# A token mixer of an FFT, a block MLP and a gated feed-forward net on one core: four chunks take their gate without a way by HBM, one sum reads PSUM, and phase one is spread over more time

## The chip, the core and the metric

The kernel runs on one core of a Trainium2 chip. Its engines are TensorE (PE: matrix products into the PSUM banks; PEld is its loading of weights), VectorE (DVE), ScalarE (ACT), GpSimd (POOL) and SyncE (SP), which here issues almost every DMA. Each engine takes its own instructions in a fixed order and waits at the head for what an instruction needs. The metric is the device time of one execution in microseconds: 1838.61 us is the median of three runs of the kernel before (1837.89 to 1843.89).

## The reference

8192 tokens of 448 channels are normalized (xn). A spectral branch s takes a Fourier transform over the tokens, a small two-layer complex MLP in four blocks of 112 channels on each frequency, a soft threshold, and the transform back. A feed-forward branch g is a gated GELU net of 1792 hidden units. The output is x + s * silu(g):

```python
xn = _layernorm(x)
Xf = rfft2(xn)                        # over 8192 tokens
hr, hi = relu(block products of Xf with w1 + b1)
or_, oi_ = softshrink(block products of h with w2 + b2, 0.01)
s = irfft2(or_ + 1j * oi_)
g = _silu((_gelu(xn @ w_gate) * (xn @ w_up)) @ w_down)
return x + s * g
```

## The kernel before

All products run in float16 pairs (a high and a low part), so that one product of the reference is three matmuls on PE. Two streams of work share the engines.

**The feed-forward stream** (`ffn`, `chunk`, `unit`, `down2`) is cut into 16 chunks of 512 tokens (`NG`), each passed twice: the first pass (p = 0) does 8 of the 14 blocks of 128 hidden units, the second (p = 1) the other 6. The first pass leaves its partial result in HBM (`prt`), the second reads it back into buffers `pt`. The tokens come transposed from HBM (`xts` into `xta`, `xtb`). A unit is two blocks of hidden units; its products come by a scheme with seven products in place of eight, called a1, a5, a6, a2, a3, a7 and a4 (in the last unit of a second pass a7 comes before a3). Their sums build up in PSUM banks `bx` (two of them) and `by`: a1, a6, a7 and a4 add into the same bank `bx`, and between two of them ACT or DVE must have read the bank's state. After a7 that is `c22` (L1097): ACT copies the bank into `v`, and then DVE or POOL adds `u` (product a5's sum) to it. a4 may add into the bank only when that copy is done. a4 is issued after the next unit's a1 and a5, or, for the last unit of a second pass, right behind a3. After a4, ACT's GELU, DVE's products and sums (`wt`, `h`) and the down products `down2` into banks `bd` and `by` follow.

At the end of a second pass the 512 x 448 result comes in four quarters (`QS`, L1213). `ended2` (L1284) adds the last sum to `pt`, takes `th` = tanh on ACT, makes the gate (th + 1) * q on DVE and writes it to HBM (`gsp<-th`). The buffers `th` are a ring of two (L490); the first pass uses the same ring for its way to HBM (`ended`, L1337, `prt<-th`). A buffer is free when its store has landed.

**The spectral stream** has three phases. Phase one (`chunk1`, L600) normalizes a chunk, writes its factors to `xts` and does the first stage of the transform into `t1`; chunk c starts at T1 + (c - 2) * DT in the plan. Phase two (`phase2`, L1725) is 64 groups of 4 frequencies and one block: transform, MLP, threshold, first stage back, into `t2`. Phase three (`phase3`, L1791) is 32 pieces of 256 tokens: `load3` (L1746) loads `u`, `mt`, `x` and the gate `g` (from `gsp`), `tiles3` (L1763) does six matmuls `bf<-u,mt` of 448 columns, multiplies on DVE with the gate, adds x (DVE or POOL) and stores (`out<-g`). Chunk 15 has no way by HBM even before: its four tiles are kept in `s4` with x in `x4l`, and `ended2` finishes them.

**Order.** The instruction streams are made ahead of time by a planner (`Pace`): every task is a generator, and the planner's own costs decide in which order tasks issue to each engine, and, for an add on SBUF alone (`Either`, L204), whether DVE or POOL takes it. Phase two is given the plan time up to `END2` = 1480, phase three up to `END3` = 1780. All instructions are recorded in one helper, so every row of the profile has its line, L199; tiles tell them apart.

Of the kernel before, what the change touches and what calls it, by code (L numbers as in the profile page):

```python
# [14 lines left out]
ALU = mybir.AluOpType  # L15
# [358 lines left out]
def afno_geglu_kernel(ctx, tc, x, gu, wd, mlp, b1, b2, c_m, c_mt, c_small, out):  # L374
# [22 lines left out]
    def ring(pool, shape, dt, name, bufs):  # L397
        return Ring(pace, pool, shape, dt, name, bufs)
# [88 lines left out]
    V1 = ring(fp, [128, 512], F32, "v1", 1)  # L487
    V2 = ring(fp, [128, 512], F32, "v2", 2)
    GL = ring(fp, [128, 512], F32, "gl", 1)
    TH = ring(fp, [128, D], F32, "th", 2)  # L490

    def load_x(c):
        x4 = EV["x4", c] = yield from X4.get()
# [146 lines left out]
            if c + 1 < NG + PL:  # L640
                yield ev("phase", c)

    T1, DT = 84.0, 40.0


    def gu_loads(fs, again):
# [346 lines left out]
                         start=first and e == 0 and n == 0, stop=last and e == 1 and n == len(seq) - 1,  # L993
                         skip_group_check=True)

    state = {}

    def scaled(p, f0):

# [23 lines left out]
    def unit(p, i, f0, h, xa):  # L1023
# [72 lines left out]

        def c22():  # L1097
            m["v2"] = yield from V2.get()
            S.copy(m["v2"], m["X"])
            pace.set(m["ev2"])  # L1100
            yield
            B.tensor_add(m["v2"], m["v2"], m["p5"])
            U5.put(m["p5"])
            yield
            pace.set(m["ec22"])
# [100 lines left out]
    def blk(a, hh, dd):  # L1206

        return a[:, hh:CH:2, DH * dd:DH * dd + DH]

    def chunk_of(a, i):  # L1210
        return a[i].rearrange("p (a d) -> p a d", a=CH)
# [31 lines left out]
    def add2(i, q, bank_):  # L1243

        yield ev("pt", i, q)
        t = EV["ptb", i, q]
        V.scalar_tensor_tensor(t, part(bank_, 128, 2, DH), cB[1], t, op0=ALU.mult, op1=ALU.add)
        yield

    def down2(i, h, last):  # L1250
# [30 lines left out]

        state["tail"] = tail

    def ended2(i, qq, b, R):  # L1284

        yield from add2(i, qq, b)
        if R:
            R.put(b)
        else:
            done("u3", i)  # L1290
        q = EV["ptb", i, qq]
        tf = yield from TH.get()
        th = tf.rearrange("p (a d) -> p a d", a=2)
        S.activation(th, q, AF.Tanh)
        yield
        if i < NG - 1:
            V.scalar_tensor_tensor(th, th, 1.0, q, op0=ALU.add, op1=ALU.mult)
            PT.put(q)
            yield
            Q.dma_start(blk(chunk_of(gsp, i), *qq), th)  # L1300
            TH.put(tf)
            EV["gn", i] = EV.get(("gn", i), 0) + 1
            if EV["gn", i] == 4:
                done("gsp", i)
            return
        for a in range(qq[0], CH, 2):
            yield ev("s4", a)
        s4, x4 = (blk(t, *qq) for t in state["last"])
        V.tensor_tensor(s4, q, s4, op=ALU.mult)
        V.scalar_tensor_tensor(th, th, 1.0, s4, op0=ALU.add, op1=ALU.mult)  # L1310
        V.tensor_add(th, th, x4)
        PT.put(q)
        yield
        Q.dma_start(blk(ov[:, CH * i:CH * i + CH, :], *qq), th)
        TH.put(tf)
# [78 lines left out]
    def chunk(p, i):  # L1394
# [10 lines left out]
        if p == 1 and nxt:  # L1405
            pace.spawn(xt_load(nxt[1], "a", nxt[0]))
        xa = EV["xta", p, i]
        if p == 1:
            pace.spawn(pt_loads(i))
        prev = None  # L1410
        for u in range(nf // 2):
            six, last = unit(p, i, 2 * u, h, xa)
# [350 lines left out]
    def tiles3(c):  # L1763
        yield ev("l3", c)
        t = EV["l3t", c]
        u2, mt = t[0:2]
        o2 = t[3] if c < 2 * NG - 2 else None
        for a in range(2):
            b = yield from BF.get()
            p = part(b, 128, D)  # L1770
            three(p, mt[:, a], u2[:, a, 0:D], u2[:, a, D:2 * D])
            yield
            if o2 is None:
                S.activation(state["last"][0][:, 2 * (c % 2) + a, :], p, AF.Copy, scale=cF)
                BF.put(b)
                yield
                done("s4", 2 * (c % 2) + a)
                continue
            V.scalar_tensor_tensor(o2[:, a, :], p, cF, o2[:, a, :], op0=ALU.mult, op1=ALU.mult)
            BF.put(b)  # L1780
            yield
            B.tensor_add(o2[:, a, :], o2[:, a, :], t[2][:, a, :])
            yield
        P3["u2"].put(u2)
        P3["mt"].put(mt)
        if o2 is not None:
            P3["x2"].put(t[2])
            Q.dma_start(ov[:, 2 * c:2 * c + 2, :], o2)
            P3["g2"].put(o2)

    def phase3():  # L1791
        r2.close()
        p3 = ctx.enter_context(tc.tile_pool(name="p3", bufs=1, side="right"))
        state["last"] = [p3.tile([128, CH, D], F32, name=n) for n in ("s4", "x4l")]
        for name, shape, dt, bufs in (("u2", [128, 2, 2 * D], F16, 3), ("mt", [128, 2, 3, 128], F16, 3),
                                      ("x2", [128, 2, D], F32, 3), ("g2", [128, 2, D], F32, 3)):
            P3[name] = ring(p3, shape, dt, name, bufs)
        n3 = 2 * NG
        order = list(range(n3))
        t0 = pace.now  # L1800
        dt = (END3 - t0 - 12.0) / n3
        pace.spawn(load3(order[0]))
        pace.spawn(load3(order[1]))
        Q.dma_start(state["last"][1], xv[:, CH * (NG - 1):, :])
        for k, c in enumerate(order):
            yield t0 + 10.0 + k * dt
            if k + 2 < n3:
                pace.spawn(load3(order[k + 2]))
            pace.spawn(tiles3(c))
# [162 lines left out]
```

## Time and profile before

| what | value |
|---|---|
| time, median of 3 runs | 1838.61 us (1837.89 to 1843.89) |
| the profiled execution | 1839.94 us |
| its span in the trace | 1838.2 us |
| PE busy | 1779.2 us (97%), 15649 matmuls |
| DVE busy | 1417.2 us (77%) |
| ACT busy | 1100.8 us (60%) |
| POOL busy | 477.4 us (26%) |
| DMA | 287.78 MB, some 300 GB/s from about 1520 to 1745 us |

A row of a timeline gives the start and the length in us, the engine, the line, the operation, the tiles as out<-in, the shape, a count, and in square brackets how long the engine was idle ahead of it and what ended that. A row of waits gives who waited for whom: total us, times, the longest. A row of grouped instructions gives, behind the first bar, the busy us and the mean ns of one. A row of windows gives the busy us of each engine in that stretch with the number of instructions, the granted PE clock, the busy share of the DMA engines and GB/s.

### The profile page before, as it was taken

To read this page: it belongs to the slowest core of one execution; us is meant where nothing else is said; L and a number is where in the kernel's file an instruction comes from. 1 tells how busy PE (TensorE), PEld (TensorE's weight loads), DVE (VectorE), ACT (ScalarE), POOL (GpSimd) and SP (SyncE) were. 2 spreads that over 40 slices of the span, in tenths; PEclk is the share of its full clock that TensorE was granted. 3 is DMA by queue.
4 is the path that set the end of the run, shared out by engine and by line. 5 is a ranking of instruction groups with operands and counts; after the bars stand their busy time and mean duration, and the time that the engine had idled before them with its cause. 6 is when DMAs were issued, how large, how long until landed. Compare 5 with 4: busy or idle time off the path is not lost. (4 is left out here: it accounts for less than half of the span.)

```text
span 1838.2 us, 39083 instructions
## 1 busy us (share of the span) xinstructions
PE 1779.2 (97%) x15649; PEld 1427.1 (78%) x15649; DVE 1417.2 (77%) x2503; ACT 1100.8 (60%) x2105; POOL 477.4 (26%) x544
## 2 busy tenths in 40 slices
PE   6999999999999999999999999999999999999997
PEld 3446677666777777887877899999999997788886
DVE  7876888777876656666767788888888877888877
ACT  4645666556665545566766777777677753444453
POOL 3232334225232112000000232333223322322222
PEclk9899999999999999999999999999999999999999
DMA  6454665676636623314236544434354359999972
GB/s 248 140 160 128 185 199 158 205 237 191 177 113 174 180 70 98 66 48 96 56 102 190 137 113 117 117 88 115 92 116 110 91 134 313 299 306 304 304 217 71
DMA packets 345654, 287.78 MB, mean 157 GB/s; under 512 B 231840, under 2 KB 312736, under 8 KB 345472
## 3 DMA queue, kind: packets, MB, share of 16 engines
q1 hardware_dynamic: 345328, 285.26, 54.4%
q8 instruction: 122, 2.00, 0.4%
q14 instruction: 60, 0.49, 0.1%
q10 hardware_dynamic: 144, 0.03, 0.0%
HBM read 129.47 MB, written 106.61 MB: 128 GB/s over the span
## 5 line engine op out<-in xcount | busy, mean ns | idle before, releaser
L199 PEld LDWEIGHTS <-wt 128*128 128x128 f16 x9350 | 911.3, 98 | 188.0 <-issue 23.3
L199 PE MATMUL bx<-xta,wt 128*128 128x256 f16 (+1 forms) x3843 | 475.4, 275 | 5.6 <-ACT th L199 3.6
L199 PEld LDWEIGHTS <-h 128*128 128x128 f16 x2688 | 257.8, 98 | 139.4 <-DVE h L199 8.5
L199 PE MATMUL bd<-dw,h 128*128 128x448 f16 (+1 forms) x1920 | 346.6, 329 | 8.3 <-DVE h L199 5.7
L199 PE MATMUL by<-xtb,wt 128*128 128x256 f16 x2080 | 251.5, 273 | 0.8 <-ACT u L199 0.8
L199 PE MATMUL by<-xta,wt 128*128 128x256 f16 (+1 forms) x1347 | 180.1, 283 | 4.9 <-DVE wt L199 3.1
L199 ACT COPY v<-bx 128x512 f32<-128x512 f32 x208 | 121.5, 584 | 99.2 <-PE bx L199 98.4
L199 POOL TENSOR_TENSOR wt<-wt 128x256 f32<-128x256 f32 x94 | 77.3, 823 | 285.0 <-DVE wt L199 263.4
L199 PE MATMUL bx<-xtb,wt 128*128 128x256 f16 x1040 | 131.6, 274 | 3.4 <-ACT v L199 3.4
L199 DVE TENSOR_TENSOR u<-by,u 128x512 f32<-128x512 f32 x104 | 71.4, 686 | 67.7 <-PE by L199 67.4
L199 ACT ACTIVATE u<-u,fc 128x512 f32<-128x512 f32 (+1 forms) x118 | 77.6, 669 | 54.9 <-DVE u L199 54.6
L199 PE MATMUL bd<-dw,wt 128*128 128x224 f16 (+1 forms) x816 | 97.1, 268 | 6.0 <-DVE pt L199 6.0
L199 POOL TENSOR_TENSOR zs<-t,zs 112x256 f16<-112x256 f32 (+1 forms) x36 | 30.7, 852 | 267.9 <-ACT zs L199 254.4
L199 ACT CAST h<-wt 128x512 f16<-128x512 f32 (+1 forms) x128 | 68.5, 537 | 37.6 <-DVE wt L199 25.1
L199 ACT COPY u<-by 128x512 f32<-128x512 f32 x104 | 60.9, 585 | 42.0 <-PE by L199 34.5
L199 DVE SCALAR_TENSOR_TENSOR pt<-bd,fb,pt 128x448 f32<-128x448 f32 x96 | 64.0, 678 | 27.3 <-PE bd L199 26.8
L199 PE MATMUL bf<-w2t,wn 112*128 112x112 f16 x1512 | 84.9, 213 | 0.0
L199 ACT ACTIVATE th<-bd,fb 128x448 f32<-128x448 f32 x62 | 39.2, 632 | 71.9 <-PE bd L199 50.1
L199 ACT COPY u<-bx 128x512 f32<-128x512 f32 x104 | 60.8, 585 | 35.7 <-PE bx L199 34.2
L199 PEld LDWEIGHTS <-wn 112*128 112x128 f16 x1512 | 80.5, 98 | 2.1
L199 ACT ACTIVATE th<-pt 128x448 f32<-128x448 f32 x64 | 36.8, 575 | 73.9 <-DVE pt L199 55.3
L199 DVE TENSOR_TENSOR v<-by,v 128x512 f32<-128x512 f32 x104 | 71.0, 683 | 9.9 <-PE by L199 9.2
(206 smaller groups left out, 3107.5 us busy)
## 6 DMA issues: line engine op xcount, KB each, us to landing
wst<-in_gu SPq DMA_DIRECT2D x22, 704.0 KB, 5.0
xts<-sx SPq DMA_DIRECT2D x32, 480.0 KB, 3.4
x<-in_x SPq DMA_DIRECT2D x17, 896.0 KB, 6.1
t<-ysb SPq DMA_DIRECT2D x64, 224.0 KB, 3.2
prt<-th SPq DMA_DIRECT2D x64, 224.0 KB, 2.1
pt<-prt SPq DMA_DIRECT2D x64, 224.0 KB, 4.1
u<-t SPq DMA_DIRECT2D x32, 448.0 KB, 6.0
y<-t SPq DMA_DIRECT2D x30, 448.0 KB, 3.6
```

Source lines behind the costliest of these rows:

```text
L199: return self.pace.issue(self.name, kind, out, ins, lambda: fn(out, *args, **kw))
```

## The change

Five things change.

- `TH` has three buffers in place of two.
- In `c22` one DVE instruction adds the PSUM bank and `u` into `v`; the ACT copy and the add behind it are gone. a4 now waits for that DVE instruction.
- `DT` is 44 in place of 40: the chunks of phase one start later, the last by 4 * 15 = 60 in plan time, and phase two with them. `END2` and `END3` stay.
- When phase three opens, chunks of the second pass that have not begun are noted as direct (`state["direct"]`); in the changed program that is chunks 11 to 14. Phase three then does 22 pieces for chunks 0 to 10 and the two of chunk 15, 24 in all. For a direct chunk, `load_gate` loads u, mt and x, `gate_bank` does the matmuls for a quarter (224 columns), and `gate` multiplies, adds x in the buffer `th` itself and stores it to the output. Nothing of these chunks goes by `gsp`.
- The rings `u2`, `mt` and `x2` have four buffers in place of three, shared by pieces and direct chunks; `g2` has two in place of three; `x4l` is gone, and chunk 15's x comes by `load_gate`.

What the planner makes of it, at three places. First, ACT in the middle of phase one, where the first pass begins. `th<-bx` and `th<-bd` evict a down product into the ring `th`; `wt_81<-cb` is weight preparation. Before:

```order
L199 ACTIVATE th<-bd,fb 128x448
L199 ACTIVATE wst<-wst,fc 128x640
L199 ACTIVATE th<-bd,fb 128x448
L199 ACTIVATE wt_81<-cb,fc 128x1024
L199 ACTIVATE th<-bx,fb 128x448 x2
L199 ACTIVATE wst<-wst,fc 128x640
L199 COPY u_1531<-bx 128x512
```

And in the changed kernel:

```order
L199 ACTIVATE wst<-wst,fc 128x640
L199 ACTIVATE th<-bd,fb 128x448 x2
L199 ACTIVATE th<-bx,fb 128x448
L199 ACTIVATE wt_81<-cb,fc 128x1024
L199 COPY u_1518<-bx 128x512
L199 ACTIVATE th<-bx,fb 128x448
```

The first eviction of a `bx` bank has moved ahead of the weight preparation. Second, DVE at the last unit of a second pass in phase three (`u<-by,u` follows a2, `v<-by,v` follows a3, the row between them with two `v` and `u` names is c22). Before:

```order
L199 TENSOR_TENSOR u_21699<-by,u_21699 128x512
L199 TENSOR_TENSOR g_21607<-g_21607,x_21511 128x448
L199 TENSOR_TENSOR wt_82<-wt_83,wt_82 128x512
L199 TENSOR_TENSOR v_21795<-v_21795,u_21715 128x512
L199 TENSOR_TENSOR v_21753<-by,v_21753 128x512
```

And at such a place in the changed kernel:

```order
L199 TENSOR_TENSOR wt_83<-wt_83 128x256
L199 TENSOR_TENSOR u_22097<-by,u_22097 128x512
L199 TENSOR_TENSOR wt_83<-wt_83 128x256
L199 TENSOR_TENSOR v_22170<-bx,u_22110 128x512
L199 TENSOR_TENSOR wt_82<-wt_83,wt_82 128x512
L199 TENSOR_TENSOR v_22138<-by,v_22138 128x512
```

The sum now reads `bx`, and one short instruction stands between it and `u<-by,u`. Third, SP in phase three, where it issues loads and stores in one queue. Before:

```order
L199 DMA_TRANSPOSE xta<-xts 128x16x256
L199 DMA gsp<-th 256x1x224
L199 DMA pt<-prt 128x2x224
L199 DMA g_21380<-gsp 128x896
L199 DMA out<-g_21190 128x896
```

And in the changed kernel, at a direct chunk's end:

```order
L199 DMA_TRANSPOSE xta<-xts 128x16x256
L199 DMA g_21702<-gsp 128x896
L199 DMA pt<-prt 128x2x224
L199 DMA out<-th 128x2x224
L199 DMA out<-g_21587 128x896
L199 DMA u_21761<-t 128x2x896
```

A store of a quarter to the output stands where the store to `gsp` stood. The diff:

```diff
--- before.py
+++ after.py
@@ -487,7 +487,7 @@
     V1 = ring(fp, [128, 512], F32, "v1", 1)
     V2 = ring(fp, [128, 512], F32, "v2", 2)
     GL = ring(fp, [128, 512], F32, "gl", 1)
-    TH = ring(fp, [128, D], F32, "th", 2)
+    TH = ring(fp, [128, D], F32, "th", 3)
 
     def load_x(c):
         x4 = EV["x4", c] = yield from X4.get()
@@ -640,7 +640,7 @@
             if c + 1 < NG + PL:
                 yield ev("phase", c)
 
-    T1, DT = 84.0, 40.0
+    T1, DT = 84.0, 44.0
 
 
     def gu_loads(fs, again):
@@ -993,7 +993,8 @@
                          start=first and e == 0 and n == 0, stop=last and e == 1 and n == len(seq) - 1,
                          skip_group_check=True)
 
-    state = {}
+
+    state = {"direct": NG}
 
     def scaled(p, f0):
 
@@ -1096,10 +1097,8 @@
 
         def c22():
             m["v2"] = yield from V2.get()
-            S.copy(m["v2"], m["X"])
+            V.tensor_tensor(m["v2"], m["X"], m["p5"], op=ALU.add)
             pace.set(m["ev2"])
-            yield
-            B.tensor_add(m["v2"], m["v2"], m["p5"])
             U5.put(m["p5"])
             yield
             pace.set(m["ec22"])
@@ -1281,8 +1280,49 @@
 
         state["tail"] = tail
 
+    def load_gate(i):
+
+        for hh in range(2):
+            sl = slice(CH * i + hh, CH * i + CH, 2)
+            t = EV["lgt", i, hh] = []
+            for k, src in (("u2", t2[sl].rearrange("n r j c -> (r j) n c")),
+                           ("mt", c_mt.rearrange("p (n s r) -> p n s r", s=3, r=128)[:, sl]), ("x2", xv[:, sl, :])):
+                if i < NG - 1 or k == "x2":
+                    t.append((yield from P3[k].get()))
+                    Q.dma_start(t[-1], src)
+            yield
+            done("lg", i, hh)
+
+    def gate_bank(i, qq):
+        hh, dd = qq
+        yield ev("lg", i, hh)
+        u2, mt = EV["lgt", i, hh][0:2]
+        b = EV["gbb", i, qq] = yield from BF.get()
+        for a in range(2):
+            three(part(b, 128, 2, DH)[:, a], mt[:, a], u2[:, a, DH * dd:DH * dd + DH],
+                  u2[:, a, D + DH * dd:D + DH * dd + DH])
+        yield
+        done("gb", i, qq)
+
+    def gate(i, qq, th):
+
+        hh, dd = qq
+        yield ev("gb", i, qq)
+        V.scalar_tensor_tensor(th, part(EV["gbb", i, qq], 128, 2, DH), cF, th, op0=ALU.mult, op1=ALU.mult)
+        BF.put(EV["gbb", i, qq])
+        yield
+        t = EV["lgt", i, hh]
+        B.tensor_add(th, th, t[2][:, :, DH * dd:DH * dd + DH])
+        yield
+        EV["gn", i, hh] = EV.get(("gn", i, hh), 0) + 1
+        if EV["gn", i, hh] == 2:
+            for k, v in zip(("u2", "mt", "x2"), t):
+                P3[k].put(v)
+
     def ended2(i, qq, b, R):
 
+        if state["direct"] <= i < NG - 1:
+            pace.spawn(gate_bank(i, qq))
         yield from add2(i, qq, b)
         if R:
             R.put(b)
@@ -1297,6 +1337,11 @@
             V.scalar_tensor_tensor(th, th, 1.0, q, op0=ALU.add, op1=ALU.mult)
             PT.put(q)
             yield
+            if i >= state["direct"]:
+                yield from gate(i, qq, th)
+                Q.dma_start(blk(ov[:, CH * i:CH * i + CH, :], *qq), th)
+                TH.put(tf)
+                return
             Q.dma_start(blk(chunk_of(gsp, i), *qq), th)
             TH.put(tf)
             EV["gn", i] = EV.get(("gn", i), 0) + 1
@@ -1305,7 +1350,8 @@
             return
         for a in range(qq[0], CH, 2):
             yield ev("s4", a)
-        s4, x4 = (blk(t, *qq) for t in state["last"])
+        yield ev("lg", i, qq[0])
+        s4, x4 = blk(state["last"], *qq), EV["lgt", i, qq[0]][-1][:, :, DH * qq[1]:DH * qq[1] + DH]
         V.tensor_tensor(s4, q, s4, op=ALU.mult)
         V.scalar_tensor_tensor(th, th, 1.0, s4, op0=ALU.add, op1=ALU.mult)
         V.tensor_add(th, th, x4)
@@ -1405,8 +1451,11 @@
         if p == 1 and nxt:
             pace.spawn(xt_load(nxt[1], "a", nxt[0]))
         xa = EV["xta", p, i]
+        state["chunk"] = p, i
         if p == 1:
             pace.spawn(pt_loads(i))
+            if state["direct"] <= i:
+                pace.spawn(load_gate(i), pace.now + 10.0)
         prev = None
         for u in range(nf // 2):
             six, last = unit(p, i, 2 * u, h, xa)
@@ -1771,7 +1820,7 @@
             three(p, mt[:, a], u2[:, a, 0:D], u2[:, a, D:2 * D])
             yield
             if o2 is None:
-                S.activation(state["last"][0][:, 2 * (c % 2) + a, :], p, AF.Copy, scale=cF)
+                S.activation(state["last"][:, 2 * (c % 2) + a, :], p, AF.Copy, scale=cF)
                 BF.put(b)
                 yield
                 done("s4", 2 * (c % 2) + a)
@@ -1791,17 +1840,17 @@
     def phase3():
         r2.close()
         p3 = ctx.enter_context(tc.tile_pool(name="p3", bufs=1, side="right"))
-        state["last"] = [p3.tile([128, CH, D], F32, name=n) for n in ("s4", "x4l")]
-        for name, shape, dt, bufs in (("u2", [128, 2, 2 * D], F16, 3), ("mt", [128, 2, 3, 128], F16, 3),
-                                      ("x2", [128, 2, D], F32, 3), ("g2", [128, 2, D], F32, 3)):
+        state["last"] = p3.tile([128, CH, D], F32, name="s4")
+        for name, shape, dt, bufs in (("u2", [128, 2, 2 * D], F16, 4), ("mt", [128, 2, 3, 128], F16, 4),
+                                      ("x2", [128, 2, D], F32, 4), ("g2", [128, 2, D], F32, 2)):
             P3[name] = ring(p3, shape, dt, name, bufs)
-        n3 = 2 * NG
-        order = list(range(n3))
+        n = state["direct"] = state["chunk"][1] + 1
+        order = [*range(2 * n), 2 * NG - 2, 2 * NG - 1]
+        n3 = len(order)
         t0 = pace.now
         dt = (END3 - t0 - 12.0) / n3
         pace.spawn(load3(order[0]))
         pace.spawn(load3(order[1]))
-        Q.dma_start(state["last"][1], xv[:, CH * (NG - 1):, :])
         for k, c in enumerate(order):
             yield t0 + 10.0 + k * dt
             if k + 2 < n3:
```

## The prediction, before the result was known

> **What bounds the kernel now.** I read the page's totals first, then PE's waits, then the timeline at the longest of them.
>
> ```profile
> PE 1779.2 (97%) x15649; PEld 1427.1 (78%) x15649; DVE 1417.2 (77%) x2503; ACT 1100.8 (60%) x2105; POOL 477.4 (26%) x544
> ...
> PE   6999999999999999999999999999999999999997
> ```
>
> PE is busy 1779.2 of 1838.2 us: 59.0 us are left, and the first two of the 40 slices (92 us, mostly start-up, which the change doesn't touch) hold a good part of it. Busy PE is dense here, as two successive rows of a timeline show:
>
> ```profile
> 1710.66 2.78 PE L199 MATMUL bx<-xta,wt 128*128 128x256 f16 x24
> 1713.28 1.47 PE L199 MATMUL by<-xta,wt 128*128 128x256 f16 x12
> ```
>
> 24 matmuls start within 2.62 us, 109 ns each. So only two things can change the time: PE's work, and the waits that end PE's idle time. PE's work hardly changes: a direct chunk's gates need 24 matmuls of 224 columns for 12 of 448, half as wide and twice as many; by columns the same, and even at 5 ns of fixed cost each the 48 more in four chunks are 0.2 us. DVE, ACT, POOL and DMA count only where PE waits for them:
>
> ```profile
> PE bd L199 <- DVE pt L199: 7.2, 19, 1.4
> PE bd L199 <- DVE h L199: 6.0, 7, 1.4
> ...
> PE bx L199 <- ACT th L199: 3.6, 1, 3.6
> PE bx L199 <- ACT v L199: 3.4, 1, 3.4
> ...
> PE bx L199 <- ACT u L199: 1.9, 2, 1.5
> ```
>
> **Term 1: the third buffer of TH.** The last three rows are one story. Here are the places, with ACT's rows ahead of them:
>
> ```profile
> 164.09 1.15 ACT L199 ACTIVATE wt<-cb,fc 128x1024 f16<-128x1024 f32 x1 [1.69 <-DVE cb L199]
> 165.14 1.14 ACT L199 ACTIVATE th<-bx,fb 128x448 f32<-128x448 f32 x2
> ...
> 165.81 1.66 PE L199 MATMUL bx<-xta,wt 128*128 128x256 f16 x12 [3.62 <-ACT th L199]
> ...
> 456.03 0.63 ACT L199 ACTIVATE th<-bd,fb 128x448 f32<-128x448 f32 x1 [2.38 <-DMA prt<-th]
> ...
> 457.19 1.47 PE L199 MATMUL bx<-xta,wt 128*128 128x256 f16 x12 [1.50 <-ACT u L199]
> ...
> 1562.04 0.58 ACT L199 ACTIVATE th<-pt 128x448 f32<-128x448 f32 x1 [6.01 <-DMA gsp<-th]
> ...
> 1563.14 2.29 PE L199 MATMUL bx<-xtb,wt 128*128 128x256 f16 x10 [3.42 <-ACT v L199]
> ```
>
> At 456 and 1562 ACT stands at the head of its queue for a `th` buffer whose store has not landed, with the copies that PE needs queued behind. At 165 the planner, short of a buffer, put the eviction behind a weight preparation that waited for DVE; in the changed order it stands ahead of it. These three waits sum to 3.62 + 1.50 + 3.42 = 8.5 us. Two of them cost more:
>
> ```profile
> 167.00:170.40 3.40, 3.40 (x18) 2.35 (x16) 2.74 (x10) 0.92 (x3) 2.88 (x5) 0.51 1.00 282
> 1563.00:1566.40 3.40, 3.26 (x16) 2.27 (x16) 1.63 (x4) 2.27 (x5) 0.00 (x0) 0.50 1.05 392
> 1682.50:1685.90 3.40, 3.29 (x18) 2.69 (x19) 2.27 (x5) 0.64 (x3) 0.73 (x1) 0.50 0.97 152
> ```
>
> The granted clock (the third number from the end) is 0.5 for 3.4 us right behind the first and the third: 1.7 us lost each. All of it is 8.5 + 3.4 = 11.9 us. At 165 something stays: two evictions (0.63 us each in ACT's rows of `th`) come first and the bank's own is still needed, say 0.9 us. With three buffers the fourth quarter still waits for the first's store, which ends its products well ahead of the others. I take **-10 us**, between 0 (the planner's new order only moves the stalls) and -11.9.
>
> **Term 2: the sum straight from PSUM.** What a c22 costs on its engines, and what it was:
>
> ```profile
> L199 ACT COPY v<-bx 128x512 f32<-128x512 f32 x208 | 121.5, 584 | 99.2 <-PE bx L199 98.4
> ...
> L199 DVE TENSOR_TENSOR v<-by,v 128x512 f32<-128x512 f32 x104 | 71.0, 683 | 9.9 <-PE by L199 9.2
> ...
> L199 DVE TENSOR_TENSOR v<-v,u 128x512 f32<-128x512 f32 x80 | 61.7, 771 | 4.0 <-ACT v L199 3.6
> ```
>
> Half of the 208 copies go: 104 x 0.584 = 60.7 us off ACT. The new add has the form of `v<-by,v`, 683 ns: 104 x 0.683 = 71.0 us for the 61.7 us that 80 adds took on DVE (24 were on POOL): +9.3 us on DVE. None of it is PE's time by itself. What counts is a4, behind DVE's queue now in place of ACT's. For most units a1 and a5 stand between a7 and a4, 24 matmuls or 2.6 us, enough. At the last unit of a second pass only a3 does:
>
> ```profile
> 1626.10 1.47 PE L199 MATMUL bx<-xta,wt 128*128 128x256 f16 x12
> 1627.41 1.26 PE L199 MATMUL by<-xtb,wt 128*128 128x256 f16 x10
> 1628.50 1.26 PE L199 MATMUL bx<-xtb,wt 128*128 128x256 f16 x10
> ...
> 1627.61 0.59 ACT L199 COPY v<-bx 128x512 f32<-128x512 f32 x1 [1.25 <-PE bx L199]
> ...
> 1627.50 0.67 DVE L199 TENSOR_TENSOR u<-by,u 128x512 f32<-128x512 f32 x1
> 1628.09 0.87 DVE L199 TENSOR_TENSOR g<-g,x 128x448 f32<-128x448 f32 x1
> ...
> 1629.48 0.68 DVE L199 TENSOR_TENSOR v<-v,u 128x512 f32<-128x512 f32 x1
> ```
>
> a7 ends at about 1627.5, ACT, idle, has copied by 1628.2, and a4 starts at 1628.50 with nothing lost. DVE is behind here: it got to the add at 1629.48. One short add of that form takes 0.41 us where POOL is idle:
>
> ```profile
> 1588.04 0.41 DVE L199 TENSOR_TENSOR wt<-wt 128x256 f32<-128x256 f32 x1
> ```
>
> In the changed order just such an add stands between `u<-by,u` and the sum, so it would start at 1627.50 + 0.6 + 0.4 = 1628.5 and end at 1629.2: a4 waits 0.7 to 0.8 us, and everything after it. By the order, the covers between a7 and a4 for the last units of chunks 10 to 14 hold 15, 10, 10, 10 and about 13 matmuls, so up to five such waits: +4 us. In phase two, PE's matmuls of the groups lie between (some 2 us of cover), +1 us for late ones. I take **+5 us**, between 0 (DVE is on time) and +12 (the sum stays as late as the add at 1629.48, 1.6 us in each of five, and the eleven other last units lose 0.4 us).
>
> **Term 3: direct chunks and the later start of phase three.** Sixteen stores of 224 KB and eight loads of 448 KB leave, 7.3 MB.
>
> ```profile
> gsp<-th SPq DMA_DIRECT2D x60, 224.0 KB, 3.3
> ...
> g<-gsp SPq DMA_DIRECT2D x30, 448.0 KB, 5.4
> ...
> 1020.00:1480.00 460.00, 457.10 (x4980) 421.26 (x4979) 393.41 (x678) 339.37 (x694) 147.57 (x144) 1.00 0.44 109
> 1520.00:1745.00 225.00, 212.69 (x1861) 181.80 (x1860) 185.31 (x281) 89.83 (x159) 61.49 (x61) 0.98 0.98 304
> ```
>
> At 304 GB/s, 7.3 MB are 24 us of a DMA system that is 98% busy in phase three. But the order, counted with 109 ns per 256 columns, puts phase three's first matmul behind 37 us more of PE work than before, so the rest has as much less time: the DMA stays about as full, and I expect little from the bytes alone. The window rows tell what the shift is worth: in phase two with second passes PE loses 2.9 of 460 us, in phase three 12.3 of 225, 5.5 us in 100. Some 37 us that turn from the second kind into the first are worth 37 x (0.055 - 0.006) = 1.8 us. The gate's two DVE instructions per quarter are those that the pieces lose. **-2 us**, between -5 and 0 here.
>
> **Term 4: DT.** The input of the first pass has slack for it:
>
> ```profile
> 628.27 0.77 SPq L199 DMA_DIRECT2D xts<-sx  x1
> ...
> 895.06 4.86 SPq L199 DMA_TRANSPOSE xta<-xts  x1
> ```
>
> Chunk 15's factors are stored at 628 and read at 895; 52 us later is still early. Counted in the same way, phase two starts some 62 us later on PE's stream and its groups stand denser, five to each second-pass chunk, against 4.7 on average. With the ACT copies gone and DVE at 393 of 460 us there, I take **0**, between -3 and +4: five groups bring 6% more of the groups' DVE work, in a chunk that is itself 1 us longer.
>
> **The sum:** 1839.94 (this execution) - 10 + 5 - 2 + 0 = 1832.9. The execution was 1.3 us above the median of the runs, so against 1838.61: **1831.6 us**.
>
> **Rivals.** (B) *The wait moves from ACT to DVE.* Term 2 at its upper end, +12, takes all that term 1 gives: 1838.61 - 10 + 12 - 2 = **1838.6**. For it: DVE is 77% busy against ACT's 60%, and DVE's lateness in phase three (1.3 us in the row at 1629.48) is real. Against it: the changed order puts fewer DVE instructions ahead of the sum.
>
> (C) *Slower: the pieces' rings run dry.* A direct chunk holds two of the four buffers of u, mt and x for most of a chunk, and g2 has two. A piece's next-but-one load of g then needs the store of the buffer to land and then the load, 5.4 us in the row above; the store's median, and the longest landing of a `th` store:
>
> ```profile
> out<-g SPq DMA_DIRECT2D x30, 448.0 KB, 4.7
> ...
> DMA to landing us min/median/max: 1.9/2.6/9.3
> ```
>
> The cycle of two pieces is about 2 x 255 / 24 = 21 us. With an estimated 4 us of work that leaves room, unless landings take 8.5 us each and more, as the 9.3 did. Past that point DVE stands at `g<-bf,ms,g`, and with it everything that PE waits for. If 8 of 24 pieces come 2 us late: 1831.6 + 16 = **1848**. Against it: no DVE wait for a g load shows in this trace's phase three.
>
> (D) *Phase three gets smooth.* The two kinds of waits at chunk ends in phase three, of which this is one, are due to the pieces' work between them on DVE:
>
> ```profile
> 1680.87 0.37 PE L199 MATMUL bd<-dw,h 128*128 128x224 f16 x2 [1.20 <-ACT h L199]
> 1682.61 0.93 PE L199 MATMUL bd<-dw,h 128*128 128x224 f16 x4 [1.37 <-DVE h L199]
> ```
>
> If the new order spreads that work, half of the 7.2 + 6.0 us of `pt` and `h` waits could go: 1831.6 - 6.6 = **1825**. Against it: DVE's work is not less.
>
> These two rows matter otherwise too. They stand right ahead of the third half-clock window above: two waits of 2.57 us in sum were enough for 1.7 us more. So new waits of 0.7 us beside them could bring such windows where there were none; five of them would be 8.5 us, inside (B). [...]
>
> **How the numbers follow.** Forecast 0.48, B 0.22, C 0.16, D 0.14. The forecast's own range is 1827 to 1836. To hold 8 in 10 the range takes in D and B and part of C: **1822 to 1844**. A change of under 0.3%, 5.5 us, can't be told from none, so faster is below 1833.1 and slower above 1844.1. Faster: 0.38 of the forecast's 0.48, D, and 0.02 of B, 0.54. Slower: 0.12 of C, 0.02 of B, 0.14. Within: 0.32.
>
> **What would show it.** Right: no PE wait on ACT `th`, `u` or `v` over 1 us, no half clock near 165 and 1560, waits of PE `bx` on DVE `v` of about 0.7 us at last units, some 5 us in all. Wrong: those waits at 10 us, or DVE waiting for `g<-gsp` or `x<-in_x`, or a new long wait in phase two.

## The result, and the profile after

| kernel | median of its runs | profiled execution | span |
|---|---|---|---|
| before | 1841.03 us (1837.89 to 1843.89, 4 runs) | 1839.94 | 1838.2 |
| changed | 1818.31 us (1815.86 to 1818.75, 4 runs) | 1818.75 | 1817.0 |

The ratio is 0.9874, with a 95% interval of 0.9852 to 0.9897. The change makes the kernel faster by some 23 us (21.2 us between the two profiled spans). That is the direction forecast, but three times the gain, and below the low end of the range (1822).

The totals of the changed kernel, and PE's waits in it (us in all, times, longest):

```profile
PE 1772.8 (98%) x15697; PEld 1429.0 (79%) x15697; DVE 1407.3 (77%) x2511; ACT 1057.0 (58%) x2001; POOL 449.6 (25%) x536
```

```profile
PE bd L199 <- DVE pt L199: 5.0, 12, 1.2
...
PE bx L199 <- ACT u L199: 2.5, 2, 1.8
...
PE bx L199 <- DVE v L199: 1.2, 3, 0.6
PE bd L199 <- ACT th L199: 1.1, 1, 1.1
...
PE bd L199 <- DVE h L199: 0.8, 1, 0.8
...
PE bx L199 <- ACT th L199: 0.2, 1, 0.2
```

The span fell by 21.2 us: PE is busy for 6.4 us less (most of it three half-clock windows of 1.7 us that are gone) and idle for 14.8 us less. Where the idle time went shows in windows laid along the stages. The bounds are the end of start-up at 92 us, the opening of phase two (the first `bf<-sm,y`, less 4 us), the first second pass, and the opening of phase three (the first `bf<-u,mt`); the columns are the length and then the busy us of PE, PEld, DVE, ACT and POOL, the clock, the DMA share and GB/s. Before:

```profile
92.00:720.00 628.00, 617.46 (x4542) 444.70 (x4541) 475.09 (x863) 360.91 (x644) 197.41 (x261) 1.00 0.57 164
...
1054.00:1523.00 469.00, 465.31 (x5034) 429.04 (x5033) 401.28 (x691) 338.82 (x692) 149.45 (x147) 1.00 0.46 114
1523.00:1838.20 315.20, 290.20 (x2546) 248.81 (x2543) 250.73 (x384) 127.51 (x225) 80.52 (x79) 0.97 0.83 256
```

Changed:

```profile
92.00:778.00 686.00, 679.99 (x5009) 489.54 (x5008) 496.08 (x900) 362.43 (x641) 176.26 (x257) 1.00 0.54 156
...
1026.00:1556.00 530.00, 525.84 (x5709) 484.13 (x5708) 461.04 (x801) 379.98 (x762) 156.21 (x155) 1.00 0.43 109
1556.00:1817.00 261.00, 247.35 (x2248) 217.65 (x2245) 217.90 (x345) 102.37 (x177) 66.10 (x69) 0.99 0.85 274
```

Length less PE's busy time is its idle time: 10.5 us against 6.0 in phase one, 3.7 against 4.2 in phase two beside second passes, 25.0 against 13.6 in phase three. Phase three is the larger part, though it opens 33 us later. Of the 4.5 us in phase one, 3.4 are the one wait on `th` at 165, term 1's. PE's waits at chunk ends within phase three, before (first two rows) and changed:

```profile
PE bd L199 <- DVE pt L199: 5.7, 13, 1.4
PE bd L199 <- DVE h L199: 4.2, 5, 1.4
```

```profile
PE bd L199 <- DVE pt L199: 4.4, 9, 1.2
PE bd L199 <- DVE h L199: 0.8, 1, 0.8
```

At a place like the one that the prediction quoted, the last unit of a second pass in phase three, the changed kernel reads like this:

```profile
1651.45 0.69 DVE L199 TENSOR_TENSOR u<-by,u 128x512 f32<-128x512 f32 x1 [0.39 <-PE by L199]
...
1652.06 0.42 DVE L199 TENSOR_TENSOR wt<-wt 128x256 f32<-128x256 f32 x1
...
1652.56 1.25 PE L199 MATMUL by<-xtb,wt 128*128 128x256 f16 x10
...
1652.83 0.69 DVE L199 TENSOR_TENSOR v<-bx,u 128x512 f32<-128x512 f32 x1 [0.36 <-PE bx L199]
...
1653.65 1.26 PE L199 MATMUL bx<-xtb,wt 128*128 128x256 f16 x10
...
1654.45 0.68 DVE L199 TENSOR_TENSOR v<-by,v 128x512 f32<-128x512 f32 x1
```

DVE itself waits, 0.39 us for `by` and 0.36 us for `bx`. The sum ends at 1653.52, and a4 starts behind a3's ten matmuls at 1653.65 with nothing lost. `v<-by,v` follows at 1654.45, 1.9 us behind a3's start; in the kernel before, DVE only came to the sum 2.1 us after a3's start.

### The profile page after: what moved, and what is told of

Same layout as the page of the kernel before. It is cut to its first block, busy times and chain, and to the rows that moved or that the text cites. A ratio compares the mean times of both kernels' runs of the same rounds, so it can differ in the third digit from the quotient of the medians.

```text
span 1817.0 us, 39056 instructions
## 1 busy us (share of the span) xinstructions
PE 1772.8 (98%) x15697; PEld 1429.0 (79%) x15697; DVE 1407.3 (77%) x2511; ACT 1057.0 (58%) x2001; POOL 449.6 (25%) x536
## 5 line engine op out<-in xcount | busy, mean ns | idle before, releaser
L199 PEld LDWEIGHTS <-wt 128*128 128x128 f16 x9350 | 908.0, 98 | 179.5 <-issue 17.6
L199 PE MATMUL bd<-dw,h 128*128 128x448 f16 (+1 forms) x1920 | 341.6, 329 | 2.7 <-ACT th L199 1.1
L199 POOL TENSOR_TENSOR wt<-wt 128x256 f32<-128x256 f32 x90 | 73.0, 812 | 347.7 <-DVE wt L199 330.5
L199 ACT COPY v<-bx 128x512 f32<-128x512 f32 x104 | 60.9, 585 | 59.6 <-PE bx L199 58.9
L199 POOL TENSOR_SCALAR st<-st 128x4 f32<-128x4 f32 x34 | 9.9, 293 | 275.2 <-DVE st L199 273.6
L199 DVE TENSOR_TENSOR v<-bx,u 128x512 f32<-128x512 f32 x104 | 70.9, 682 | 4.6 <-PE bx L199 4.2
```

The lines of the kernel that those rows point to most:

```text
L199: return self.pace.issue(self.name, kind, out, ins, lambda: fn(out, *args, **kw))
```

## The experiments

T is the third `th` buffer, S the sum from PSUM, G the direct chunks with their rings, D DT 44. "Opens" is the first `bf<-u,mt` of the profiled execution. "Late pieces" are the pieces of phase three whose products begin after 1800 us, when the feed-forward stream is ending (counted from the matmul rows, six to a piece). The idle times are PE's, by windows as above; phase three's includes 8 us and more behind the last matmul. Each time stands beside that of the kernel before on the same chip. "us per group" is the mean distance between the starts of phase two's groups (the first of each twelve `bf<-sm,y` matmuls), from the first second pass to the last group. With G, the number of direct chunks follows the opening: five where phase three opens by 1542, four at 1553 to 1580, three from 1591 on. The profiled executions of t_only and s_only are the fastest of their ten runs, 4 us under the median, so their rows don't show what the median loses.

| run | parts, DT / END2 | median us | before | opens | us per group | late pieces | idle in phase one | two, second passes | three |
|---|---|---|---|---|---|---|---|---|---|
| before | none, 40/1480 | 1838.61 | | 1523 | 11.30 | 1 | 10.5 | 3.7 | 25.0 |
| t_only | T, 40/1480 | 1843.17 | 1839.33 | 1536 | 11.43 | 0 | 15.0 | 6.8 | 20.3 |
| s_only | S, 40/1480 | 1842.89 | 1839.33 | 1527 | 11.39 | 0.7 | 13.5 | 6.5 | 22.1 |
| g_only | G, 40/1480 | 1833.30 | 1839.33 | 1524 | 11.30 | 0 | 11.5 | 3.7 | 20.0 |
| d_only | D, 44/1480 | 1850.46 | 1839.33 | 1604 | 11.91 | 7.5 | 3.7 | 14.1 | 31.2 |
| no_t | SGD, 44/1480 | 1837.16 | 1838.27 | 1580 | 11.50 | 4 | 8.8 | 3.9 | 27.5 |
| no_s | TGD, 44/1480 | 1853.97 | 1838.27 | 1604 | 11.98 | 7 | 12.2 | 10.2 | 27.9 |
| no_g | TSD, 44/1480 | 1819.93 | 1838.27 | 1557 | 11.09 | 0.5 | 6.5 | 4.5 | 14.6 |
| no_d | TSG, 40/1480 | 1829.33 | 1838.27 | 1523 | 11.06 | 0 | 14.3 | 1.2 | 17.1 |
| changed | TSGD, 44/1480 | 1818.31 | 1841.03 | 1556 | 11.09 | 0 | 6.0 | 4.2 | 13.6 |
| dt42 | TSG, 42/1480 | 1824.95 | 1838.40 | 1532 | 11.39 | 0 | 4.7 | 6.5 | 15.7 |
| dt43 | TSG, 43/1480 | 1827.38 | 1838.40 | 1542 | 11.14 | 0 | 7.8 | 6.7 | 16.7 |
| dt46 | TSG, 46/1480 | 1864.41 | 1838.40 | 1610 | 11.76 | 8 | 6.7 | 9.7 | 44.9 |
| dummy_copy | TSGD and an ACT copy | 1914.27 | 1838.40 | 1637 | 12.37 | 12 | 11.2 | 17.3 | 75.3 |
| act_free | TSGD and a free ACT copy | 1916.29 | 1840.14 | 1640 | 12.37 | 12 | 9.7 | 17.3 | 73.2 |
| e1460 | TSGD, 44/1460 | 1833.77 | 1840.14 | 1591 | 11.91 | 4.5 | 5.8 | 9.9 | 21.0 |
| tg | TG, 40/1480 | 1835.74 | 1840.14 | 1537 | 11.43 | 0 | 14.9 | 6.8 | 16.0 |
| e1440_42 | TSG, 42/1440 | 1817.78 | 1840.14 | 1514 | 11.22 | 0 | 4.6 | 3.5 | 15.4 |
| b42 | none, 42/1440 | 1834.81 | 1839.33 | 1564 | 11.89 | 4 | 7.9 | 12.4 | 17.6 |
| tg42 | TG, 42/1420 | 1830.29 | 1839.33 | 1553 | 11.96 | 0 | 7.0 | 10.2 | 16.4 |

**Each part alone.** The theory was the prediction's: a sum of four terms. The rival: parts that need each other. The edits, each on the kernel before: `th` with three buffers; the new c22; all hunks on `gate`, `load_gate` and the rings; and

```diff
-    T1, DT = 84.0, 40.0
+    T1, DT = 84.0, 44.0
```

> The kernel before with three buffers TH and nothing else. All theories: the three PE waits behind ACT (165, 457 and 1563 us; 8.5 us) and the half clocks behind the first and the third (3.4 us) go, 9 to 12 us faster than before. Phase three's waits of PE on DVE h and pt at chunk ends stay (over 8 us in all), unless a buffer of th was their cause too; then 15 us or more.

> The kernel before with the sum of c22 straight from PSUM and nothing else. Theory S (the sum, no longer made of two instructions on two engines, comes earlier in DVE's queue at a second pass's last unit, and so does all behind it): the PE waits on DVE h and pt at chunk ends in phase three fall from 8 to under 4 us, and the kernel is 6 to 10 us faster, the th waits staying. The prediction's term 2: 5 us slower, by waits of PE bx on DVE v. Theory G: no change within 3 us.

> The kernel before with direct gates (and their rings) and nothing else; TH has two buffers, DT is 40. Theory G (the gates of direct chunks free phase three's DMA and spread DVE's work): phase three loses 8 us less on PE. Theory S: phase three's waits on h stay, and with two buffers that now wait for a longer way (tanh, gate, add, store) ACT's waits for th are longer than before: 0 to 5 us slower.

> The kernel before with DT 44 and nothing else. The prediction's term 4: within 4 us of before. Theory D (the new order by itself, which opens phase three one chunk and a half later, does away with waits there): 5 to 10 us faster.

T alone costs 3.8 us (ratio 1.0018, 1.0006 to 1.0030), S alone 3.6 (1.0015, 1.0004 to 1.0027), D alone 11.1 (1.0054, 1.0037 to 1.0071), and G alone gains 6.0 (0.9964, 0.9951 to 0.9977). Together that would be 12.5 us slower; the change is some 23 us faster. So the parts are not terms of a sum, and the single runs can't say what each is worth. In s_only the waits that the prediction's term 2 foresaw do stand, some 4 us of them, though only two of the five (2.1 us) are in phase three:

```profile
PE bx L199 <- DVE v L199: 4.0, 5, 1.3
```

**Each part taken out.** The same four edits, undone one at a time in the changed kernel.

> The changed kernel with two buffers TH. If the third buffer is worth what the prediction says, 9 to 12 us slower than the changed kernel, with PE waits behind ACT th back in phase one and half clocks behind them; more than 12 if direct chunks, whose th is held longer, need it even more.

> The changed kernel with the ACT copy and the add of before. Theory S: 5 to 10 us slower than the changed kernel, with PE waits on DVE h and pt at chunk ends in phase three back at some 8 us. Theory G: within 2 us of it. The prediction's term 2: 5 us faster than it.

> The changed kernel with all gates of chunks 0 to 14 by HBM, as before. Theory G: 6 to 10 us slower than the changed kernel, lost in phase three. Theory S: within 3 us of it.

> The changed kernel with DT 40. Theory D: 5 to 10 us slower. The prediction's term 4: within 4 us.

Without G the changed kernel takes 1819.93 us, 1.6 more (by the ratios to the kernel before on each chip, 0.9907 and 0.9874, some 6): with the rest in place the way by HBM costs little, though phase three then moves the bytes of 32 pieces again. Without D it takes 1829.33 (11 more), without T 1837.16 (19 more), without S 1853.97 (36 more). S and T look dear, yet all that T was to remove in the kernel before was 11.9 us, and S was to cost. The table shows what else is different: without T or S phase three opens at 1580 and 1604 us in place of 1556, with 4 and 7 pieces left after 1800. In no_s, PE waits at the end for loads of the last pieces, and at chunk ends for `h`:

```profile
PE bd L199 <- DVE h L199: 6.3, 6, 1.3
...
PE bf L199 <- DMA mt<-c_mt: 4.7, 2, 2.4
```

That formed a new theory (O): the opening of phase three decides, and the parts count through the number of groups of phase two that the planner fits beside each second-pass chunk. The changed kernel has five groups in each.

**The size of DT, and ACT's copies put back.** DT alone is varied in the changed kernel. dummy_copy adds an ACT copy behind each sum, so ACT has its 61 us again:

```diff
+            S.copy(m["p5"], m["v2"])
```

> The changed kernel with DT 42 in place of 44. Theory D (the late opening of phase two pays in phase one, by spreading its work, and its loss there falls steadily with DT: 20.5 us at 40, 8.8 at 44): about 14 us of loss in phase one, 1822 to 1825. Rival (44 is one lucky order; the stalls of phase one change from order to order by chance): the loss in phase one lies anywhere between 8 and 21 us with no order in DT.

> DT 43. Theory D: 11 us of loss in phase one, about 1820. Rival (chance): anywhere between 1815 and 1830, not between the neighbours.

> DT 46. Theory D with its other end: phase one loses a little less than at 44 (6 to 9 us), but phase two opens some 30 us later, its groups can't keep pace, phase three opens about 1580 to 1600 and ends with the pieces' loads and the last quarters: a tail of over 10 us and waits for mt, 1830 to 1845. Rival (late opening by itself costs nothing; the dear thing in the kernels without the sum or the buffer was their own stalls): 1815 to 1820.

> The changed kernel, with one ACT copy put back behind each sum, from the same PSUM bank into the same buffer that the sum has just written (it repeats no value the kernel needs: the buffer then holds X without p5, so the output is not the reference's; 104 copies of about 0.584 us, 61 us on ACT). The sum itself is still one DVE instruction straight from PSUM. Theory 1 (what the direct sum is worth is that it is early on DVE, ahead of the products that PE waits for): the last product is as early as in the changed kernel plus one copy; the time is within 6 us of it, 1818 to 1824. Theory 2 (it is worth ACT's 61 us: with them back the planner packs phase two less densely, phase three opens late and is pressed, as where the sum was undone): phase three's first matmul at about 1600 us instead of 1556, waits of PE for the pieces' loads of mt at the end, a tail of over 10 us, 1846 to 1854.

The losses of phase one in these texts are counted otherwise than the table's idle time, which is 14.3 us in no_d and 6.0 in the changed kernel. The last text describes its edit wrongly: the copy goes from the sum's buffer `v` into `u`, which holds nothing that is still needed, so no value is lost and the chain of the sum is as it was.

dt42 takes 1824.95 us and dt43 1827.38, so the gain does not grow step by step with DT: dt43 is worse than expected and dt42 at the edge. That dt43 doesn't lie between its neighbours is what the rival of chance foresaw, so nothing shows that the 44 itself is more than one good order. Phase one's idle time falls at once, from 10.5 to 15.0 us in the six kernels with DT 40 to 4.6 to 7.9 in the five with 42 or 43, and beyond that only scatters (3.7 to 12.2 in the nine with 44 or 46). dt46 loses on the other side, as expected and 19 us past the range: 1864.41. dummy_copy goes far past either expectation, 1914.27, on the side of theory 2 (ACT's load), with phase three opening at 1637.

**The opening alone, and the copy once more.** e1460 keeps every part and moves one number of the plan. act_free lets ACT copy `u` onto itself behind the sum, so the copy doesn't even read the sum; only the next use of `u` waits for it:

```diff
-    END1, END2, END3 = T1 + NG * DT + 12.0, 1480.0, 1780.0
+    END1, END2, END3 = T1 + NG * DT + 12.0, 1460.0, 1780.0
```

```diff
             V.tensor_tensor(m["v2"], m["X"], m["p5"], op=ALU.add)
             pace.set(m["ev2"])
+            S.copy(m["p5"], m["p5"])
```

tg undoes S and D; e1440_42 is the changed kernel with DT 42 and END2 1440.

> The changed kernel with END2 1460 in place of 1480, nothing else: the plan asks for the groups of phase two a little earlier, and what the planner makes of it is a pattern of 4 and 6 groups per second-pass chunk instead of 5 in each, with phase three's first matmul 30 us later on PE's stream. Theory O (the opening of phase three decides, and the three parts count through it): phase three opens at about 1587 instead of 1556, waits and a tail at the end as in the kernels without the buffer (1580) and without the sum (1604), 1832 to 1848. Rival P (the parts themselves save the time, by waits they take away at their own places): all parts are there, 1816 to 1822.

> The changed kernel with an ACT copy of the buffer u onto itself behind each sum (104 copies, some 61 us on ACT; values unchanged). Nothing but the next use of that buffer waits for it, so the chain of the sum is as short as in the changed kernel. The order on PE is exactly that of the run with the copy into the sum's buffer (phase three 60 us later on PE's stream than in the changed kernel). Theory O: that run's late opening is kept, about 1615 to 1637, and most of its loss: 1850 to 1885; the rest, up to 1914, was the longer chain. Rival (the longer chain made all of its loss): 1818 to 1826.

> The third buffer and the direct chunks alone: the changed kernel without the sum and with DT 40. Phase three's first matmul is 31 us earlier on PE's stream than in the changed kernel, phase one as unspread as before. Theory O: with an early opening the sum is worth little, so this is near the kernel without DT alone (1829.3) plus the few us of waits on h at chunk ends that the sum takes away: 1829 to 1838. Rival P (the sum saves its 36 us anywhere): about 1829 + 30 = 1855 to 1865.

> All parts, with DT 42 and END2 1440: the order has five groups in each second-pass chunk again, and phase three's first matmul 37 us earlier on PE's stream than in the changed kernel. Theory O with the loss in phase one that DT 42 had (7 us, 9 us in the changed kernel): no worse than the changed kernel, 1812 to 1820. Rival (an earlier phase three only loses more in itself, as where DT was 40, 12 us against 8): 1821 to 1826.

e1460 speaks for theory O: 1833.77 us with all parts in place (three direct chunks in place of four), 15 us more than the changed kernel, from 20 units of plan time. So having the parts is not enough. Its groups are unevenly spread and take 11.91 us each in place of 11.09, so phase three opens 35 us later. Phase one is as in the changed kernel; of the 13.2 us between the two spans, 5.7 are idle time beside the second passes, ahead of the opening, and 7.4 are idle time in phase three, as its windows show (phase one, second passes, phase three, and the end):

```profile
92.00:774.00 682.00, 676.24 (x4992) 487.88 (x4990) 492.57 (x893) 361.80 (x640) 174.09 (x253) 1.00 0.55 156
...
1024.00:1591.00 567.00, 557.15 (x5969) 510.27 (x5968) 470.78 (x814) 378.86 (x782) 174.09 (x174) 1.00 0.42 105
1591.00:1830.20 239.20, 218.13 (x1942) 187.68 (x1939) 194.60 (x308) 88.18 (x153) 65.78 (x65) 0.98 0.92 298
1800.00:1830.20 30.20, 14.44 (x113) 10.24 (x110) 21.48 (x35) 5.28 (x9) 2.40 (x3) 0.81 0.70 239
```

act_free has dummy_copy's order on PE, instruction for instruction, and its time within 2 us of it: 1916.29, so whether the copy reads the sum is nothing. The rival is out: 104 copies (64 us) on an engine that is busy 58% of the time cost 98 us, with phase three opening at 1640. That is not the price of ACT's time alone: no_s has as much of it, with the copy ahead of the sum as in the kernel before, and is 36 us dearer than the changed kernel, not 98. Here each copy stands behind DVE's sum, and ACT, which takes its instructions in order, waits there for 166 us:

```profile
L199 ACT COPY u<-u 128x512 f32<-128x512 f32 x104 | 64.3, 618 | 166.1 <-DVE v L199 166.1
```

How much of the 98 us is the load and how much the place was not tried. They are more than the 1850 to 1885 us expected, and the end of the trace says where they are lost. The first row is the window from 1800 to the end, then PE's wait for the banks of the pieces, then DVE's and SP's rows for three pairs of pieces:

```profile
1800.00:1912.30 112.30, 43.59 (x245) 26.65 (x242) 50.87 (x81) 11.03 (x19) 6.86 (x8) 0.66 0.62 215
```

```profile
PE bf L199 <- DVE g L199: 40.0, 6, 12.4
```

```profile
1823.60 0.68 DVE L199 SCALAR_TENSOR_TENSOR g<-bf,ms,g 128x448 f32<-128x448 f32 x1 [11.56 <-DMA g<-gsp]
1840.55 0.68 DVE L199 SCALAR_TENSOR_TENSOR g<-bf,ms,g 128x448 f32<-128x448 f32 x1 [11.84 <-DMA g<-gsp]
1856.87 0.68 DVE L199 SCALAR_TENSOR_TENSOR g<-bf,ms,g 128x448 f32<-128x448 f32 x1 [4.51 <-DMA g<-gsp]
```

```profile
1815.30 4.57 SPq L199 DMA_DIRECT2D g<-gsp  x2
1827.48 0.34 SPq L199 DMA_DIRECT2D out<-g  x1
1830.42 0.36 SPq L199 DMA_DIRECT2D out<-g  x1
```

Twelve pieces are left when the feed-forward stream has hardly any products to cover them. Then, for these pairs, the ring `g2` of two sets the time: load two gates, multiply for 5 us, store both, and only then load the next two. The starts are 17.0 and 16.3 us apart; DVE waits for 11.6 and 11.8 us ahead of the first two, and ahead of the third 5.5 us for a direct chunk's x and then 4.5 for g. PE is busy for 43.6 of the last 112 us.

tg, 1835.74, lies inside its 1829 to 1838: with an early opening S is worth only 6.4 us against no_d's 1829.33, or 4.5, since the kernel before was 1.9 us lower on that chip. e1440_42, 1817.78 (ratio 0.9882, 0.9865 to 0.9899), also as expected: a different DT, a different opening, the same time as the changed kernel. It doesn't beat it by anything that can be told.

**How much the plan's two numbers hold by themselves.** b42 is the kernel before with DT 42 and END2 1440, nothing else; tg42 is e1440_42 without S, with END2 1420 so that the opening stays early.

> The kernel before with two numbers of the plan changed, DT 42 and END2 1440; two th buffers, the copy and the way by HBM all kept. Phase three's first matmul stands 4 us earlier on PE's stream than in the changed kernel. Theory O with phase one's loss (14 to 20 us in six kernels at DT 40, 7 at 42): some 7 to 10 us better than before in phase one, the waits behind ACT and at chunk ends kept: 1827 to 1835. Rival P (parts): the constants bring nothing or cost, as DT alone did: 1838 to 1850.

> The run with DT 42 and END2 1440 (1817.8) without the sum from PSUM: the ACT copy and the add are back, END2 is 1420 so that phase three's first matmul stays early, 10 us ahead of the changed kernel's on PE's stream. Theory O: the sum's own worth is the few us of waits at chunk ends in phase three and of fewer groups per chunk: 1820 to 1828. Rival P (the sum is worth 20 us and more anywhere): 1838 or more.

b42 takes 1834.81 us, 4.5 better than before (0.9979, 0.9967 to 0.9991), at the upper end of what was expected. Phase one's idle time is 2.6 us less and phase three's 7.4, and the three half-clock windows are gone (a mean clock of 0.997 over the span, before 0.992), but beside the second passes it idles 8.7 us more. tg42 takes 1830.29, a miss by 2 us: S is worth 12.5 us here, not 2 to 10 (END2 differs by 20 too). It shows where the opening is not all. The two windows beside the second passes, tg42 and then e1440_42:

```profile
1041.00:1553.00 512.00, 501.75 (x5408) 460.70 (x5406) 430.44 (x747) 357.04 (x729) 155.37 (x148) 1.00 0.42 106
```

```profile
1043.00:1514.00 471.00, 467.49 (x5064) 430.44 (x5063) 403.21 (x706) 332.32 (x674) 137.50 (x137) 1.00 0.45 111
```

10.2 us idle against 3.5, 6.7 of the 10.4 us between the two spans; 2.4 are in phase one and 1.0 in phase three. The table has this for all: in the twelve kernels with up to 11.50 us per group PE idles 1 to 7 us there, in the eight from 11.76 on it idles 10 to 17. Which of the two makes the other is not shown.

What the runs leave open: a split of the gain among T, S and D. Each changes the planner's pattern, a step of 20 in END2 changes it as much, and only T, S and D together were seen to give five groups per chunk at DT 44. No run moves the opening without the pattern ahead of it. Nor was it tried by itself what makes DVE late at chunk ends, but the traces point at S: phase three's waits on DVE `h` are 2.2 to 5.7 us in the eight kernels without S, and at most 1.8 in all with it but s_only, which has 4.3.

## Why the prediction was wrong, point by point

**What bounds the kernel** was right: PE, and its waits. But the terms were summed as if each stage kept its order. Between the two profiled spans lie 21.2 us: 7.4 are waits on DVE `pt` and `h`, 5.7 waits on ACT `th` and `v`, 5.1 the three half-clock windows, and 3.0 the rest. Of these the sum had the second and two of the three windows, 9.1 us, as term 1; it had nothing for the first. That says where the time went, not which part of the change took it away.

**Term 1 (-10)** was right in the changed kernel and wrong as a price of the buffer. The waits on ACT `th` and `v` are down to 1.3 us from 7.0, the half-clock windows at 165 and 1560 are gone, and no half clock appears between start-up and 1800 (the clock is 1.00 from 65 to 1811 us). By itself the buffer brought its lower bound, 0, and less: in t_only the planner moved the stalls, phase one's idle time rose from 10.5 to 15.0 us. Waits on ACT `u` of 1.8 us and on `th` of 1.1 stand in the changed kernel too, over the 1 us that the prediction had set.

**Term 2 (+5)** has the wrong sign in the whole, and this is the step that failed first: "a4 waits 0.7 to 0.8 us" at the last units. The waits of `bx` on DVE `v` are 1.2 us in all, 0.4 of them in phase three. (With S alone the term holds, 4.0 us of these waits and 3.6 us slower, though only half of them lie in phase three.) The price of the sum was right (682 ns for 683 estimated), but its start was put together from two orders: the old start of `u<-by,u` on a DVE that was behind, and the new instruction after it. In the new order DVE is ahead of PE at the place shown and waits for the bank; in all of phase three PE waits once for the sum, 0.4 us. The larger miss is what the term left out. "None of it is PE's time by itself" was said of ACT's 61 us; with S undone (no_s) the planner's order costs 36 us more, with a later opening and waits on `h` of 6.3 us, though at DT 40 (tg against no_d) only 4.5 to 6.4.

**Term 3 (-2)** was about right in size for what was built: 1.6 us when it is taken out, or some 6 by the ratios. Its other half, that the later opening is worth 1.8 us by itself, failed: e1440_42, the changed kernel and no_g open at 1514, 1556 and 1557 us and lie within 2 us of each other, dt42 and dt43, which open between them, lie 7 and 9 us above, and every kernel with three or more of the parts that opens from 1580 on is 15 to 98 us above the changed one.

**Term 4 (0)** is the second step that failed. The start of phase two was counted well (58 us later for 62), and five groups to a chunk too. But "slack for it" looked only at what is late, not at what the spreading relieves: without D (no_d) phase one's idle time is 14.3 us, with it 6.0, and the whole is 11 us faster with it. Its upper bound, +4, was far too low as well: alone DT 44 costs 11 us. Phase two then opens as late as in the changed kernel, its groups take 11.9 us each in place of 11.1, phase three opens at 1604, and 7.5 pieces begin after 1800.

**Rivals.** (D), given 0.14, is what happened: the `pt` and `h` waits went from 13.2 to 5.8 us, 7.4 less where it had 6.6, beside term 1. Leaving these waits out of the sum is the largest step that failed. In part the near hit is luck: the 13.2 us are of the whole trace, in phase three only 9.9 stood, and there they fell by 4.7. Its objection, that DVE's work is not less, was wrong by 10 us (1417.2 to 1407.3), and beside the point: what counts is when DVE is behind, and that changed. (B) did not come. (C) did not come in the changed kernel, and act_free shows why. A pair of pieces takes 17 us from load to load there, less than the 21 us that (C) reckoned between them, so the ring `g2` sets the pace only where few other products do. In the changed kernel DVE never waits for `g<-gsp` in phase three, and no piece begins after 1800.

**The range.** Its low end, 1822, was the forecast with one rival's 6.6 us and some more. It had no case in which term 1, D and a gain from DT come together, because the four were treated as apart.

## What to carry to other kernels

Where a planner makes the order, a change's first effect is the order, and a cost per instruction can't be carried from the old one into it. Read the new order for where each stage opens and how evenly the streams are mixed, and ask what the last stage needs to be hidden behind: here three kernels that opened it between 1514 and 1557 us were equal, and the six with three or more of the parts that opened it from 1580 on were 15 to 98 us dearer, with pieces left when nothing covered them any more. Test such parts by taking them out of the whole rather than by adding them alone, and move the plan's own constants once, since 20 units of END2 moved the time by 15 us, as much as most of the parts.

## What the runs showed of the hardware

In the clock records of the kernel before, three stretches between 92 and 1790 us are at half clock. They start at 166.95, 1563.00 and 1682.47 us and are 3.413 us long each; their starts lie 1396.05 and 119.47 us apart, 409.0 and 35.0 times that length. PE's waits beside them are 3.62 us, 3.42 us and, in two parts, 2.57 us; at the wait of 1.50 us that ends at 457.19 the clock stays at 1.00. The changed kernel has no half clock between 65 and 1811 us. How long a wait is does not settle by itself what follows: the kernel before and g_only have the same wait in phase one. Before it is 2.85 us, and the clock stays; in g_only it is 2.18 us, and the clock is 0.50 for 3.4 us, an estimated 1.7 us lost by this clock and length. What sets the two apart was not shown:

```profile
332.07 0.38 PE L199 MATMUL bf<-identf,fx 128*2 128x128 f32 x2 [2.85 <-DVE fx L199]
333.30:336.70 3.40, 3.40 (x20) 1.77 (x18) 1.40 (x8) 1.82 (x5) 1.90 (x5) 1.00 1.20 315
```

```profile
332.20 0.38 PE L199 MATMUL bf<-identf,fx 128*2 128x128 f32 x2 [2.18 <-DVE fx L199]
333.30:336.70 3.40, 3.40 (x11) 1.47 (x10) 1.65 (x8) 1.29 (x4) 1.84 (x5) 0.50 1.18 307
```

The first row of each pair is PE's timeline, the second a window (0.50 is the clock).

The sum from PSUM was no dearer than the same sum from SBUF: a median of 681 ns against 685 for the old `v<-v,u`, in rows of the same form. (The old row's mean, 771, comes from some long ones, up to 1643 ns.)

```profile
L199 DVE TENSOR_TENSOR v<-bx,u 128x512 f32<-128x512 f32 x104 | 70.9, 682 | 4.6 <-PE bx L199 4.2 <-ACT wt L199 0.2
```
